# RWKV-7 recurrence and a low-rank mixer on one core: the recurrence's inverse, products and order written anew

## The chip, the core and the metric

The kernel runs on one core of one Trainium2 chip. TensorE (PE) multiplies, VectorE (DVE), ScalarE (ACT) and GpSimd (POOL) do the elementwise work, and SyncE (SP) issues the DMAs. The metric is the device time of one execution in microseconds (us), smaller is better. Everything is computed in float32.

## The reference

```python
# r, k, v, w, a, b: (4 batches, 8 heads, 768 steps, 40)
for t in range(S):
    y[t]  = r[t] @ state                      # state: (B, H, 40, 40)
    Sa    = state @ a[t]
    state = state * w[t] - outer(Sa, b[t]) + outer(v[t], k[t])
x = y as (B, 768, 320)                        # heads side by side
u = x + (x.T @ U @ V).T                       # U: (768, 32), V: (32, 768)
out = u + relu(u @ w_ch1) @ w_ch2             # (320, 1280), (1280, 320)
```

The weights of the mixer come as 64-bit floats and are turned into float32 on the core, from their halves, in pieces of 320 columns.

## The kernel before

**Units.** The steps are cut into 12 chunks of L = 64, the batches into two pairs. A *unit* is one chunk of one pair, with its 8 heads; there are N = 24 units, 0 to 11 for the first pair. Within a chunk the recurrence is written with the running product P of the decays: keys and b are divided by P, a and r multiplied by it, and the steps inside the chunk become products of 64x64 matrices per head and batch: a strictly triangular matrix is masked, the inverse T of identity minus a triangle is needed, and only the 40x40 state passes from unit to unit.

**Stages of a unit.** `prep_f` (L273) clips w, turns it (`up`, four transposes with the identity, L253), makes P by one scan of 512 columns (L289), turns P back twice (pp, pq, L258), takes 1/P with RECIPROCAL (L296), makes bt on POOL (L312), turns it and multiplies it with `fa` (`scores`, L264): `fn`, the negative triangle, which goes to DRAM (`fd`) and comes back as `ln`, with each 16x16 diagonal block on one partition, 64 lanes a unit. `substitute` inverts these blocks on POOL for two units at once: 14 steps of two operations (L348, L350). The result goes over DRAM (`TD`) and back (`fetch`) into `tc`. `prep_s` widens the inverse from 16 to 32 (pg, px, L398 and L420, 32x32 products) and from 32 to 64 (pg2, px2, L436 and L446), turns v, r and kt, and makes the masked scores `e` and `cm`. `carry` uses the state: ph (L463, L468), pX (L477), py (L485, L490), pg, pd (L509), the output py with ng (L528), which L530 multiplies by `qt` into XTM. The new state is decayed on DVE (L520), doubled on POOL into ST (L523) and turned by eight transposes into pS (L537).

**Quarters.** A product of 64 rows and 64 columns fills one quarter of the array. `scores` walks the quarters (0,0), (1,1), (0,1), (1,0); the loops over `hs` use row half x with output half x, so only two of the four.

**Order.** A generator yields between the steps, and `merged` weaves carry of unit n, prep_s of n+1, prep_f of n+5 and substitute by fixed shares; the queues of all engines follow that text:

```python
            merged(*gens)
            next(wload, None)
            if n >= 0:
                next(wload, None)
```

SP's queue in particular takes loads, fd, ln, TD and tc in this order. PSUM has four one-bank tiles and two two-bank tiles.

**Between the halves.** The squares of all inputs and outputs (L247) are counted against limits; `flag` is read by every engine (L603), and only if a limit is passed is the recurrence run again step by step (L604). It isn't in these runs. Then the mixer: `mix` (U, V, turns), `up_proj` (L729, L732) and `down_proj` (L744, L748), six groups of four units, 512 columns at a time.

Of the kernel before, what the change touches and what calls it, by code (L numbers as in the profile page):

```python
# [15 lines left out]
W_LO, W_HI = 0.6, 1.6  # L32
X_HI = 1e5
Y_HI = 1e18
# [3 lines left out]
def kernel(  # L38
# [22 lines left out]
    DP = 64  # L61
    LB = 16
    N = NB // 2 * NCH
    NCHK = 7
    NJ = DFF // 128
    WP = 320

    def half(x):
        return slice(64 * x, 64 * (x + 1))


    gl = ctx.enter_context(tc.tile_pool(name="gl", bufs=1))
    ones = gl.tile([128, 128], F32, name="ones")
    nc.vector.memset(ones[:], 1.0)
    ID = gl.tile([128, 128], F32, name="ID")
    nc.gpsimd.affine_select(out=ID[:], in_=ones[:], pattern=[[1, 128]], compare_op=ALU.is_equal,
                            fill=0.0, base=0, channel_multiplier=-1)

    MU = gl.tile([128, L], F32, name="MU")
    MF = gl.tile([128, L], F32, name="MF")  # L80
    IB = gl.tile([128, 32], F32, name="IB")
    up_ = gl.tile([128, 1], F32, name="up_")
    with tc.tile_pool(name="build", bufs=1) as bp:
        m = bp.tile([128, 128], F32, name="m")
        nc.gpsimd.affine_select(out=m[:], in_=ones[:], pattern=[[1, 128]], compare_op=ALU.is_gt,
                                fill=0.0, base=0, channel_multiplier=-1)
        f = bp.tile([128, 128], F32, name="f")
        nc.gpsimd.affine_select(out=f[:], in_=ones[:], pattern=[[LB, 128 // LB], [0, LB]],
                                compare_op=ALU.is_gt, fill=0.0, base=0, channel_multiplier=-1)
        for x in range(2):  # L90
            nc.vector.tensor_copy(MU[half(x), :], m[half(x), half(x)])
            nc.vector.tensor_copy(MF[half(x), :], f[half(x), half(x)])
    for q in range(4):
        s = slice(32 * q, 32 * q + 32)
        nc.vector.tensor_copy(IB[s, :], ID[s, s])
        nc.vector.memset(up_[s, :], 1.0 - q % 2)


    XTM = gl.tile([128, N, DM], F32, name="XTM")
    flag = gl.tile([1, 1], I32, name="flag")  # L100
    U_, V_ = gl.tile([128, NCH, RANK], F32, name="U_"), gl.tile([RANK, T], F32, name="V_")

    W1 = [gl.tile([128, DFF], F32, name=f"W1_{i}") for i in range(3)]
    W2 = gl.tile([128, NJ, DM], F32, name="W2")

    def weights(pool):

        u = moe_U.rearrange("(c p) k -> p c k", p=L)
        for c in range(0, NCH, 6):
            x = slice(c, c + 6)  # L110
            yield from piece(pool, U_[:, x, :], [(half(h), u[:, x, :]) for h in range(2)])
        for t in range(0, T, WP):
            x = slice(t, min(t + WP, T))
            yield from piece(pool, V_[:, x], [(slice(0, RANK), moe_V[:, x])])
        for f in range(0, DFF, WP):
            x = slice(f, f + WP)
            for i in range(2):
                yield from piece(pool, W1[i][:, x], [(slice(0, 128), moe_w_ch1[128 * i:128 * i + 128, x])])
            yield from piece(pool, W1[2][:, x], [(half(h), moe_w_ch1[256:320, x]) for h in range(2)])
        w2 = moe_w_ch2.rearrange("(j p) e -> p j e", p=128)  # L120
        for j in range(NJ):
            yield from piece(pool, W2[:, j, :], [(slice(0, 128), w2[:, j, :])])

    def piece(pool, dst, srcs):

        p = dst.shape[0]
        n = dst.size() // p
        if srcs[0][1].dtype == F32:  # L130
            for s, x in srcs:
                nc.sync.dma_start(out=dst[s], in_=x)
            yield
            return
        raw = pool.tile([128, WP, 2], I32, name="raw", bufs=2)
        x = raw[:, 0:n, :].rearrange("p n h -> p (n h)")
        if len(dst.shape) == 3:
            x = x.rearrange("p (j e) -> p j e", j=dst.shape[1])
            dst = dst.rearrange("p j e -> p (j e)")
        for s, y in srcs:  # L140
            nc.sync.dma_start(out=x[s], in_=y.bitcast(I32))
        yield
        raw = raw[0:p, 0:n, :]
        lo, hi = raw[:, :, 0], raw[:, :, 1]
        t = pool.tile([128, WP], I32, name="bits")[0:p, 0:n]
        e = pool.tile([128, WP], I32, name="unit")[0:p, 0:n]
        s = pool.tile([128, WP], I32, name="size")[0:p, 0:n]
        g = pool.tile([128, WP], F32, name="low")[0:p, 0:n]
        nc.scalar.activation(out=g, in_=lo.bitcast(U32), func=ACTF.Copy, scale=2.0 ** -52)  # L149
        nc.vector.tensor_scalar(out=t, in0=hi, scalar1=3, scalar2=0x3FFFFFF8,  # L150
                                op0=ALU.logical_shift_left, op1=ALU.bitwise_and)
# [6 lines left out]
                                op0=ALU.is_ge)  # L158
        nc.gpsimd.tensor_tensor(out=g, in0=t.bitcast(F32), in1=g, op=ALU.add)
        nc.gpsimd.tensor_tensor(out=dst, in0=g, in1=e.bitcast(F32), op=ALU.mult)  # L160
        yield

    with ExitStack() as p1:
# [172 lines left out]
        def substitute(u):  # L339
# [4 lines left out]
            for j in range(1, LB - 1):  # L344
# [6 lines left out]
                if j % 2:  # L351
                    yield
# [438 lines left out]
```

## Time and profile before

| | |
|---|---|
| Time, median of 3 runs | 1075.54 us (1068.68 to 1079.84) |
| Profiled execution, first to last instruction | 1071.0 us |
| PE busy | 903.6 us, 84% |
| DVE, ACT, POOL busy | 330.3, 251.7, 300.4 us |
| Mean granted PE clock | 0.835 of full |
| First and last XTM output (L530) | 95.5 and 705.2 us |
| Largest groups | L744 135.8 us, L729 111.0 us (PE) |
| DMA | 51.19 MB, 26.4% of the 16 engines |

The profile is of one execution and gives its span, not its time as the runs are timed; the runs lie around the span by what happens before the first and after the last instruction. A group of instructions is given as line, engine, output<-input, partitions x elements, count, busy time and mean. A float32 product appears as two records, a transpose as one. PE's busy time is not its speed: the granted clock beside it, in tenths of full, says how fast it ran.

### The profile page before, as it was taken

How to read it: one execution, taken by the hardware profiler on the slowest of the kernel's cores; microseconds unless marked ns; L12 is line 12 of the kernel's file. 1: busy time of each engine (PE TensorE's matmuls, PEld its weight loads, DVE VectorE, ACT ScalarE, POOL GpSimd, SP SyncE). 2: the span in 40 equal slices, each digit the busy share in tenths (PEclk: the TensorE clock that was granted, in tenths of full speed). 3: DMA queues.
4: the chain of work that ended last, by engine and by line, in shares of the span. 5: the costliest groups of instructions: out<-in, count | busy, mean ns of one | idle time of the engine just before them, and what ended most of it. 6: DMA issues, size and time to landing. Idle time of an engine off the chain costs nothing. (4 is left out here: it accounts for less than half of the span.)

```text
span 1071.0 us, 33742 instructions
## 1 busy us (share of the span) xinstructions
PE 903.6 (84%) x15146; PEld 675.0 (63%) x15146; DVE 330.3 (31%) x668; ACT 251.7 (23%) x630; POOL 300.4 (28%) x616
## 2 busy tenths in 40 slices
PE   2558789888788888888997868978989999999988
PEld 2447688777677787776886857853636455454635
DVE  5534334354434445443434214111111110101010
ACT  1223333333433343333333323200000000000010
POOL 5434524453625353525244446000000000000000
PEclk9656777787868787867779668669999999999999
DMA  4464342535252525443525221000000001010001
GB/s 97 70 96 80 50 85 42 95 48 99 45 99 45 96 48 99 70 73 51 94 42 91 51 61 27 3 3 0 13 13 13 12 1 25 1 24 1 22 3 25
DMA packets 262500, 51.19 MB, mean 48 GB/s; under 512 B 256112, under 2 KB 259216, under 8 KB 262352
## 3 DMA queue, kind: packets, MB, share of 16 engines
q1 hardware_dynamic: 262352, 49.01, 26.4%
q8 instruction: 119, 1.95, 0.7%
q14 instruction: 29, 0.24, 0.1%
HBM read 36.11 MB, written 12.86 MB: 46 GB/s over the span
## 5 line engine op out<-in xcount | busy, mean ns | idle before, releaser
L744 PE MATMUL p<-W,hid 128*128 128x320 f32 x480 | 135.8, 438 | 0.0
L729 PE MATMUL p<-uf,W 128*128 128x512 f32 x240 | 111.0, 605 | 16.6 <-ACT hid L734 16.6
L744 PEld LDWEIGHTS p<-W,hid 128*128 128x128 f32 x480 | 89.2, 190 | 45.3 <-issue 11.3
L729 PEld LDWEIGHTS p<-uf,W 128*128 128x128 f32 x240 | 43.1, 189 | 82.3 <-issue 45.8
L734 ACT ACTIVATE hid<-p 128x512 f32<-128x512 f32 x30 | 17.9, 597 | 324.1 <-PE p L732 324.1
L537 PE MATMUL pS<-ID,ST 128*128 128x128 f32 x176 | 43.9, 419 | 35.0 <-POOL ST L523 35.0
L296 DVE RECIPROCAL ip<-pp 128x320 f32<-128x320 f32 x24 | 51.8, 2158 | 46.1 <-PE pp L258 46.0
L735 DVE TENSOR_SCALAR hid<-p 128x512 f32<-128x512 f32 x30 | 20.8, 692 | 139.4 <-PE p L732 139.4
L537 PEld LDWEIGHTS pS<-ID,ST 128*128 128x128 f32 x176 | 35.2, 221 | 37.1 <-POOL ST L523 36.8
L436 PE MATMUL pg<-tt,fm 32*64 32x32 f32 x768 | 43.1, 277 | 13.1 <-DVE tt L428 11.6
L751 DVE TENSOR_TENSOR o<-p,XTM 128x320 f32<-128x320 f32 x24 | 11.8, 492 | 136.8 <-PE p L748 136.8
L436 PEld LDWEIGHTS pg<-tt,fm 32*64 32x64 f32 x768 | 40.0, 203 | 17.5 <-PE px L420 8.1
L156 POOL TENSOR_TENSOR low<-low,unit 128x320 f32<-128x320 f32 (+3 forms) x27 | 22.4, 829 | 100.9 <-ACT low L149 75.9
L350 POOL TENSOR_TENSOR ln<-ln,tmp 128x14 f32<-128x14 f32 (+6 forms) x168 | 45.4, 271 | 11.9
L348 POOL TENSOR_TENSOR tmp<-ln 128x14 f32<-128x14 f32 (+6 forms) x168 | 44.7, 266 | 12.7
L150 DVE TENSOR_SCALAR bits<-raw 128x320 int32<-128x320 int32 (+3 forms) x27 | 17.1, 634 | 96.4 <-DMA raw<-in_moe_w_ch_dram 75.2
L287 DVE COPY seg<-pw 128x8 f32<-128x8 f32 x24 | 4.1, 171 | 132.5 <-PE pw L253 132.5
L523 POOL TENSOR_TENSOR ST<-sc,slot 128x640 f32<-128x640 f32 x22 | 27.6, 1255 | 57.8 <-DVE sc L520 57.8
L446 PEld LDWEIGHTS px<-t,GX 32*64 32x64 f32 x768 | 39.3, 194 | 7.0 <-issue 4.8
L446 PE MATMUL px<-t,GX 32*64 32x32 f32 x768 | 43.7, 271 | 0.0
L312 POOL TENSOR_TENSOR nBT<-nB,ip 128x320 f32<-128x320 f32 x24 | 20.7, 863 | 77.3 <-DVE ip L296 72.4
L463 PE MATMUL ph<-nV,e 64*64 64x40 f32 x768 | 41.1, 282 | 0.0
(155 smaller groups left out, 1660.6 us busy)
## 6 DMA issues: line engine op xcount, KB each, us to landing
fd<-fn SPq DMA_DIRECT2D x48, 128.0 KB, 2.6
raw<-in_moe_w_ch_dram SPq DMA_DIRECT2D x18, 320.0 KB, 4.0
nW<-in_w_dram SPq DMA_DIRECT2D x48, 80.0 KB, 3.1
nA<-in_a_dram SPq DMA_DIRECT2D x48, 80.0 KB, 3.0
nB<-in_b_dram SPq DMA_DIRECT2D x48, 80.0 KB, 2.9
nR<-in_r_dram SPq DMA_DIRECT2D x48, 80.0 KB, 2.8
nK<-in_k_dram SPq DMA_DIRECT2D x48, 80.0 KB, 3.2
nV<-in_v_dram SPq DMA_DIRECT2D x48, 80.0 KB, 3.2
```

Of the source, the lines that this page charges most:

```text
L156: nc.gpsimd.tensor_tensor(out=g, in0=g, in1=e.bitcast(F32), op=ALU.mult)
L296: nc.vector.reciprocal(out=u.ip[:], in_=heads(p[:])[:, :, 0:D])
L348: nc.gpsimd.tensor_tensor(out=x, in0=ln[:, 0:j, j:j + 1].to_broadcast([128, j, n]), in1=ln[:, j:j + 1, j + 1:].to_broadcast([128, j, n]), ...
L350: nc.gpsimd.tensor_tensor(out=ln[:, 0:j, j + 1:], in0=ln[:, 0:j, j + 1:], in1=x, op=ALU.add)
L436: nc.tensor.matmul(out=pg[half(x), 32 * h:32 * h + 32], lhsT=fm[s, h, :], rhs=tt[s, h, :], start=True, stop=True)
L446: nc.tensor.matmul(out=px[half(x), 32 * h:32 * h + 32], lhsT=GX[s, h, :], rhs=t2[s, h, :], start=True, stop=True)
L463: nc.tensor.matmul(out=ph[half(x), s, i], lhsT=u.e[half(x), s, i, :], rhs=vt[half(x), 2 * i + s, 0:D], start=i + s == 0, stop=first, skip_ ...
L523: nc.gpsimd.tensor_tensor(out=ST[:, :, :, 0:D], in0=sc[:].rearrange("p i x e -> p (i x) e").unsqueeze(2).to_broadcast([128, NH, 2, D]), in ...
L537: nc.tensor.transpose(out=p[:, h // 4, 128 * (h % 4):128 * (h % 4 + 1)], in_=ST[:, h].rearrange("p s e -> p (s e)"), identity=ID[:])
L729: nc.tensor.matmul(out=ps_[x][:], lhsT=W1[i][:, (j + x) * 128:(j + x + 1) * 128], rhs=uf[i][:], start=(i == 0), stop=False)
L735: nc.vector.tensor_scalar_max(hid[:, j + 1, :], ps_[1][:], 0.0)
L744: nc.tensor.matmul(out=p[:, 0:DM], lhsT=hid[:, f, 2 * j * L:2 * (j + 1) * L], rhs=W2[:, f, :], start=(f == 0), stop=False, skip_group_chec ...
```

## The change

The recurrence, its order and the mixer are written anew; the fallback behind the flag stays.

- **Order.** Nothing is issued where it is written: each step is added to a list (`Plan.add`) with engine, planned duration, priority and buffers, and `Plan.order` runs one list schedule over all engines, PSUM places included; the queues follow it. PSUM is four pairs of banks, given out by the plan.
- **P and 1/P.** w is taken in packed rows of 320 columns; its check is one ACT pass. A backward scan gives the products of the later decays, their total is inverted (five columns), and a forward scan gives P. RECIPROCAL over 320 columns, the clip and the squares go.
- **Inverse.** 32x32 diagonal blocks lie on lanes, 32 lanes a unit, in groups of up to four units: 30 steps of two operations, on DVE for unit 0 alone, on POOL for the other seven groups. tLN and tLT have one buffer. T1 and T2 widen 32 to 64.
- **Products** of 64x64 walk all four quarters (QUADS). The state is one tile, decayed on DVE, turned by 16 products (SP).
- **Slots.** Eight sets of prepared operands, four of them in the room of W2 and of the mixer's tile MX; units 20 to 23 use the four others, so W2 is loaded after unit 15 through a single conversion buffer.
- **Mixer.** Groups of three units, 384 columns. x plus the low-rank part is written to XTM first. The half for the first pair has priority 1000, and may use up to four banks while units remain; the second half has 2000. The flag is read at the very end.

```diff
+LAT = {"PE": 160.0, "DVE": 110.0, "ACT": 130.0, "POOL": 120.0, "SP": 2500.0}
...
+                while free[e] <= t and ready[e]:
+                    pick = None
+                    for pri, n in sorted(ready[e]):
+                        o = self.ops[n]
...
+                    if e == "PE":
+                        if o.mode != mode:
+                            d += 95
+                        mode = o.mode
+                    o.start, o.end = t, t + d
+                    free[e] = o.end
...
+    pairs = [ps.tile([128, 2, 512], F32, name=f"pb{i}") for i in range(4)]
...
+    tLN, tLT = ring("tLN", 1, 1024), ring("tLT", 1, 1024)
...
+    CV = ring("CV", 1, 2 * WP, I32)
...
+    PARTS = (("aT", 512), ("NN", 512), ("KQ", 512), ("BQ", 512), ("Pn", TP))
+    SLOT = sum(c for _, c in PARTS)
+    NPERM, NSL = 4, 8
...
+    room = [[W2F, 0, NJ * DM], [MX, 0, MXC]]
...
+        return slots[n % NSL if n < 20 else n - 20]
...
+    QUADS = ((0, 0), (1, 1), (0, 1), (1, 0))
...
+    GROUPS = [[0], [1, 2, 3]] + [list(range(n, n + 4)) for n in range(4, 20, 4)] + [[20, 21], [22, 23]]
...
+        PL.add("PE", 400, f, r=[W], w=[pw], pri=pri, mode=1, name=f"wT{n}")
+        PL.add("ACT", 650, lambda: act(JK[:], W.ap[:], func=ACTF.Relu, scale=-1.0, bias=WLO[:],
+                                       accum_out=SQ[:, n:n + 1]), r=[W], w=[whole(JK), PL.buf(SQ, n, n + 1)],
...
+        PL.add("DVE", 180, lambda: nc.vector.memset(pw.ap[:, 0:NS + 1:L], 0.0), r=[pw], w=[pw], pri=pri, name=f"z{n}")
+        PL.add("DVE", 800, lambda: nc.vector.tensor_tensor_scan(
+            out=RB.ap[:, ::-1], data0=pw.ap[:, 1:NS + 1][:, ::-1], data1=C1[:, ::-1], initial=0.0,
+            op0=ALU.mult, op1=ALU.add), r=[pw], w=[RB], pri=pri, name=f"bs{n}")
+        w0 = whole(tW0)
+        PL.add("DVE", 180, lambda: nc.vector.tensor_tensor(out=tW0[:], in0=RB.ap[:, 0:NS:L], in1=WF.ap[:, 1:NS:L], op=ALU.mult),
+               r=[RB, WF], w=[w0], pri=pri, name=f"pl{n}")
+        PL.add("DVE", 180, lambda: nc.vector.reciprocal(out=D1.ap[:, 0:NS:L], in_=tW0[:]),
+               r=[w0], w=[D1], pri=pri, name=f"rc{n}")
+        PL.add("DVE", 800, lambda: nc.vector.tensor_tensor_scan(
+            out=FW.ap, data0=WF.ap, data1=D1.ap, initial=0.0,
+            op0=ALU.mult, op1=ALU.add), r=[WF, D1], w=[FW], pri=pri, name=f"fs{n}")
...
+            for y in range(2):
+                for x in range(2):
+                    mm(pp.ap[half(x), y, 0:128], FW.ap[:, 128 * x + 64 * y:128 * x + 64 * y + 64], ID[:])
+            for y in range(2):
+                for x in range(2):
+                    mm(pp.ap[half(x), y, 128:160], FW.ap[half(y), 256:320], ID[half(y), 64 * y + 32 * x:64 * y + 32 * x + 32])
+        PL.add("PE", 560, f, r=[FW], w=[pp], pri=pri, mode=1, name=f"Pn{n}")
...
+                        mm(pl.ap[half(h2), 4 * y + 2 * l:4 * y + 2 * l + 2], S["Pn"].ap[:, c0:c0 + 64], E0[:])
+        PL.add("PE", 300, f, r=[S["Pn"]], w=[pl], pri=pri + 2, mode=2, name=f"PL{n}")
...
+        turned(S["aT"], AH, pri, f"aT{n}")
+        turned(BT, S["BQ"], pri, f"BT{n}")
+        pf = P2()
+        scores_a(pf, BT, S["aT"], pri, f"F{n}")
+        masked(S["NN"], pf, MN, pri, f"NN{n}")
...
+    HEADS = [(x, y, l, h2) for x in range(2) for l in range(2) for y, h2 in QUADS]
+    HEADC = [(x, y, l, h2) for x in range(2) for h2 in range(2) for y, l in QUADS]
+
+    def scores_a(p, bt, at, pri, name):
+        def f():
+            for x, y, l, h2 in HEADS:
+                c0 = 128 * (2 * x + l)
+                mm(p.ap[half(y), h2, c0 // 2:c0 // 2 + 64], bt.ap[half(h2), 256 * l + 128 * x + 64 * y:256 * l + 128 * x + 64 * y + 64],
+                   at.ap[half(h2), 256 * y + 128 * l + 64 * x:256 * y + 128 * l + 64 * x + 64])
+        PL.add("PE", 500, f, r=[bt, at], w=[p], pri=pri, mode=3, name=name)
...
+        eng, e = (nc.vector, "DVE") if g == 0 else (nc.gpsimd, "POOL")
+        tm = whole(tTM[0])
+        for j in range(1, 31):
+            m = 31 - j
+
+            def f(j=j, m=m):
+                y = tTM[0][0:nl, 0:j * m].rearrange("p (a b) -> p a b", b=m)
+                eng.tensor_tensor(out=y, in0=x3[0:nl, 0:j, j:j + 1].to_broadcast([nl, j, m]),
+                                  in1=x3[0:nl, j:j + 1, j + 1:].to_broadcast([nl, j, m]), op=ALU.mult)
+                eng.tensor_tensor(out=x3[0:nl, 0:j, j + 1:], in0=x3[0:nl, 0:j, j + 1:], in1=y, op=ALU.add)
+            c = 400 + 3.5 * j * m if e == "POOL" else 350 + 2.0 * j * m
+            PL.add(e, c, f, r=[ln], w=[ln, tm], pri=pri - 4, name=f"lan{g}.{j}")
...
+        PL.add("POOL", 220, lambda: nc.gpsimd.memset(ln.ap[0:nl, 0:1024:33], 1.0), r=[ln], w=[ln], pri=pri - 4, name=f"dg{g}")
+        PL.add("ACT", 1150, lambda: act(lt.ap[0:nl].rearrange("l (t j) -> l t j", j=32),
+                                        x3[0:nl].rearrange("l j t -> l t j")), r=[ln], w=[lt], pri=pri - 4, name=f"LT{g}")
+        gd = gdram[g % 2]
+        gdb = gd_buf[g % 2]
+        for blk, s in ((1, ln), (0, lt)):
+            PL.add("SP", 430, lambda blk=blk, s=s: dma(
+                gd[0:nl // 2, blk].rearrange("l j t -> l (j t)"), s.ap[blk:nl:2]),
+                r=[s], w=[gdb], pri=pri - 4, grp=("gd", g), name=f"gd{g}")
...
+            for h in range(NH):
+                for x in range(2):
+                    s = slice(64 * x, 64 * x + 32)
+                    mm(p.ap[half(x), 32 * h:32 * h + 32], S["NN"].ap[s, 64 * h:64 * h + 64], AB.ap[s, 32 * h:32 * h + 32])
+        PL.add("PE", 500, f, r=[S["NN"], AB], w=[p], pri=pri, mode=4, name=f"T1.{n}")
...
+        for h2 in range(2):
+            p = P2()
+
+            def f(h2=h2, p=p):
+                for i in range(4):
+                    h = 4 * h2 + i
+                    for y in range(2):
+                        for blk in range(2):
+                            rows = slice(64 * y + 32 * blk, 64 * y + 32 * blk + 32)
+                            mm(p.ap[half(h2 ^ y), blk, 32 * i:32 * i + 32], LT2.ap[rows, 64 * h:64 * h + 64],
+                               ID[rows, rows] if blk == 0 else AB.ap[rows, 32 * h:32 * h + 32])
+            PL.add("PE", 330, f, r=[LT2, AB], w=[p], pri=pri, mode=4, name=f"T2.{n}.{h2}")
...
+        turned(KT, S["KQ"], pri, f"KT{n}")
+        pe, pc = P2(), P2()
+        scores_a(pe, KT, S["aT"], pri, f"E{n}")
+        masked(E, pe, MU, pri, f"mE{n}")
+        turned(VT, V, pri, f"VT{n}")
+        turned(RT, R, pri, f"RT{n}")
+        scores_r(pc, lambda x, y, l, h2: 128 * (2 * x + h2) + 64 * y, VT, RT, pri, f"C{n}")
+        masked(C, pc, MU, pri, f"mC{n}")
+
...
+                        mm(ph.ap[half(q), y, D * i:D * i + D], S["aT"].ap[half(h2), a0:a0 + 64],
+                           ST.ap[half(h2), 160 * y + D * i:160 * y + D * i + D])
+            PL.add("PE", 400, f, r=[S["aT"], ST], w=[ph], pri=pri, mode=3, name=f"H{n}")
+            PL.add("DVE", 520, lambda: nc.vector.scalar_tensor_tensor(
+                out=nh, in0=ph.ap[:, :, 0:160], scalar=-1.0, in1=ne, op0=ALU.mult, op1=ALU.add),
+                r=[ph, NE], w=[NHh], pri=pri, name=f"eH{n}")
...
+            for t, z in ((C, S["KQ"]), (G, S["BQ"])):
+                for l in range(2):
+                    for h2 in range(2):
+                        for x, y in QUADS:
+                            c0, k0 = 256 * l + 64 * (2 * x + h2), 256 * l + 128 * x + 64 * h2
+                            mm(py.ap[half(x), y, 80 * l + D * h2:80 * l + D * h2 + D], t.ap[half(y), c0:c0 + 64],
...
+            PL.add("DVE", 500, lambda: decay(st4, pd.ap[:, :, 0:160].rearrange("p s (i d) -> p s i d", d=D)),
+                   r=[pd, pls], w=[ST], pri=pri, name=f"S0.{n}")
+        else:
+            PL.add("DVE", 420, lambda: decay(st4, SN.ap.rearrange("p (s i d) -> p s i d", s=2, d=D)),
...
+                    mm(p.ap[32 * gq:32 * gq + 32, x, 0:DM], U_[half(x), c, :], XTM[half(x), pr * NCH + c, :],
+                       start=c < 4, stop=c >= 8)
+        PL.add("PE", 2000, f, r=bU + [xtm[n] for n in units], w=[p], pri=pri, mode=5, name=f"ph{pr}")
...
+                        mm(p.ap[half(x), y, 0:DM], V_[s, (c + y) * L:(c + y + 1) * L], hut.ap[s, DM * x:DM * x + DM])
+            n0 = pr * NCH + c
+            PL.add("PE", 700, f, r=bV + [hut], w=[p], pri=pri + 0.01 * c, mode=6, name=f"V{pr}.{c}")
...
+                            mm(p.ap[:, y, 0:GN], W1[i][:, (j + y) * 128:(j + y + 1) * 128], ufs[i].ap, start=i == 0, stop=False)
+                        prev = (PL.add("PE", 650, f, r=[ufs[i]] + [bW1[x, i] for x in fs], w=[p], pri=q + 0.02, mode=0,
+                                       grp=("up", pr, g, j), name=f"up{pr}.{g}.{j}", after=prev),)
+
+                def f(j=j, p=p):
+                    for y in range(2):
+                        mm(p.ap[:, y, 0:GN], W1[2][half(y), (j + y) * 128:(j + y + 1) * 128], ufs[2].ap[half(y)], start=False)
+                PL.add("PE", 700, f, r=[ufs[2]] + [bW1[x, 2] for x in fs], w=[p], pri=q + 0.02, mode=7, grp=("up", pr, g, j),
+                       name=f"up{pr}.{g}.{j}", after=prev)
...
+                        mm(p.ap[:, 0:DM], hid.ap[:, f_ * GN + 128 * jj:f_ * GN + 128 * jj + 128], W2[:, f_, :],
+                           start=f_ == 0, stop=f_ == NJ - 1)
+                    prev = (PL.add("PE", 545, f, r=[hidj[f_ // 2], bW2[f_]], w=[p], pri=q + 0.04, mode=0, grp=("dn", n),
+                                   name=f"dn{n}", after=prev),)
...
+    for g, us in enumerate(GROUPS):
+        for u, n in enumerate(us):
+            q = us[0] - 4.6 + 0.35 * u
+            load(n, "WABK", q - 1)
+            prep_f(n, q, lane[n])
+        lanes(g, us[0] - 4.6)
+        if g == 0:
+            weights1(1.0, 0.8)
+        if us[0] == 16:
+            weights2(16.0, 0.5)
+        for n in us:
+            load(n, "VR", n - 2.5)
+            prep_t(n, lane[n], n - 1.5)
+            prep_s(n, n - 1.2)
+            carry(n, n)
+        if us[-1] == 19:
+            mixer(0, 1000.0, True)
+    mixer(1, 2000.0, True)
+
...
+    steps, span = PL.order(4, 4)
+    global PLAN
+    PLAN = PL, steps, span
+    with tc.manual_schedule():
+        for o in steps:
+            o.fn()
+    main.close()
...
-            for i, s, x in hs:
-                nc.tensor.matmul(out=ph[half(x), s, i], lhsT=u.e[half(x), s, i, :], rhs=vt[half(x), 2 * i + s, 0:D],
-                                 start=i + s == 0, stop=first, skip_group_check=True)
...
-        for n in range(-AH, N):
...
-            merged(*gens)
...
-    uf = mix(0)
-    for g in range(NG):
-        hid = up_proj(uf)
-        if g + 1 < NG:
-            uf = mix(g + 1)
-        down_proj(g, hid)
```

## The prediction

> **What bounds the kernel now.** I read the forty slices first, then cut the span where the work changes, then looked at single blocks of TensorE.
>
> ```profile
> PE   2558789888788888888997868978989999999988
> PEclk9656777787868787867779668669999999999999
> ```
>
> PE is busy nearly everywhere, but its clock has two regimes: 0.6 to 0.8 up to slice 26, 0.9 and more after it. The cuts of the second view are the first output of a unit (95.5 us), the last one (705.2), and the first matmul of the mixer (711.2):
>
> ```profile
> core 0: us, PE busy (x) PEld busy (x) DVE busy (x) ACT busy (x) POOL busy (x), PEclk, DMA share, GB/s
> 95.50:705.20 609.70, 515.88 (x13084) 459.26 (x13084) 237.01 (x483) 206.77 (x530) 257.85 (x498) 0.76 0.37 63
> 0.00:95.50 95.50, 48.58 (x812) 41.53 (x812) 44.75 (x102) 26.99 (x70) 42.58 (x118) 0.75 0.51 87
> 705.20:711.20 6.00, 0.19 (x2) 0.09 (x2) 1.51 (x8) 0.00 (x0) 0.00 (x0) 0.50 0.02 5
> 711.20:1071.00 359.80, 338.95 (x1248) 174.14 (x1248) 47.03 (x76) 17.92 (x30) 0.00 (x0) 0.99 0.05 11
> ```
>
> So 1071.0 = 95.5 lead + 609.7 for 23 further units (26.5 each) + 6.0 for flag and branch + 359.8 mixer. No other engine is over 43% in the second row, and the mixer is TensorE at full clock. The waits of PE between 100 and 700 us are small but for one:
>
> ```profile
> PE pS L537 <- POOL ST L523: 35.0, 11, 9.1
> PE pd L509 <- DVE ng L269: 12.2, 16, 0.8
> PE px L420 <- issue: 11.6, 9, 2.1
> PE pg L436 <- DVE tt L428: 10.6, 10, 1.2
> ```
>
> The price of a block is its start to the next start, at the full clock and at the half clock (columns: start, length, then the group):
>
> ```profile
> 230.75 0.66 PE L258 MATMUL pp<-ID,PF 128*128 128x128 f32 x4
> 231.24 0.60 PE L258 MATMUL pq<-ID,PF 128*128 128x128 f32 x4
> 231.77 0.69 PE L264 MATMUL pg<-fr,xf 64*64 64x64 f32 x32
> 232.28 0.65 PE L264 MATMUL pe<-fa,fk 64*64 64x64 f32 x32
> 232.75 0.65 PE L264 MATMUL pe<-fr,fv 64*64 64x64 f32 x32
> ...
> 694.11 1.93 PE L463 MATMUL ph<-nV,e 64*64 64x40 f32 x32
> 695.97 1.33 PE L468 MATMUL ph<-ST,fa 128*64 128x80 f32 x16
> ```
>
> A product is two records. At the full clock four transposes take 0.49, and 16 products on all four quarters 0.47. The same 16 in `hs` order, which meets only the two diagonal quarters, took 1.06 (py at 228.98 to 230.04) and at the half clock 1.86 (the ph row). The other full-clock starts: pd 0.49 per 16 products, ph and py with 80 columns 0.6 to 0.7, pg and px of 32x32 blocks 0.8, pg2 and px2 on two row groups 1.05.
>
> **TensorE work of a unit, at the full clock.** Before: 44 transposes 11 x 0.49 = 5.4; five score blocks and pX 2.35; pd 1.0; ph, py, py again 3.2; the 80-column products 1.3; pg, px 1.6; pg2, px2 2.1: 16.9 us. The chip spent 515.9/23 = 22.4 busy us on it, a factor 1.33 (clock 0.76), and 26.5 of span, another 1.18 of waits.
>
> After: prep_f: aT, BT 1.0; wT, Pn, Q, each two transposes or four half-width products and four small ones, 0.45 to 0.5; the PL pairs 0.5 (below); F 0.47: 3.4. prep_t: T1 has L446's two row groups and half its products (16 for two blocks of 8): by that row 1.05, T2 two four-quarter blocks 0.95: 2.0. prep_s: three turns, E, C: 2.4. carry: He, H, X, XT, G, Yr, SP seven at 0.47, Y and S two each: 5.2. Sum 13.0, with first and last chunks shorter 12.8. So 24 units cost 307 us at the full clock instead of 406: 99 less, or 132 at this stage's clock. The doubtful items: PL (16 records with two columns) lies between 0.2 (records at the 14.5 ns spacing of L264) and 0.7 (the 80-column row), I take 0.5; T1 between 0.47 and 1.9 (L436 at the half clock), I take 1.05; reversed operands in the scan: none in the trace, between nothing and a second 1.22 us of DVE, which is hidden.
>
> **The clock: rule against row.** The Trainium skill, "TensorE: Matmul & The Clock Gate", Part 1, says that the array reaches full rate after about one busy window of 3.4 us; a denser stage would then pay no 1.33. The trace disagrees for these small products:
>
> ```profile
> 456.00:466.00 10.00, 10.00 (x164) 9.10 (x165) 2.98 (x8) 4.54 (x11) 3.07 (x5) 0.72 0.55 85
> 483.00:503.00 20.00, 18.55 (x480) 16.64 (x472) 7.80 (x14) 6.55 (x17) 10.33 (x28) 0.77 0.37 58
> ```
>
> PE is 100% and 93% busy there, at 0.72 and 0.77. By the rule units cost 12.8 x 1.09 = 14.0, by the row 12.8 x 1.33 x 1.09 = 18.6. I take the row. The 1.09 for waits is my choice, half of the 1.18: the ST wait (35 of about 90 us) goes, since the state is made on DVE and needs no doubled ST and no pS; the other hops stay.
>
> **What is hidden.** POOL:
>
> ```profile
> L350 POOL TENSOR_TENSOR ln<-ln,tmp 128x56 f32<-128x56 f32 x24 | 7.4, 308 | 1.9
> L350 POOL TENSOR_TENSOR ln<-ln,tmp 128x14 f32<-128x14 f32 x24 | 5.2, 218 | 1.1
> L348 POOL TENSOR_TENSOR tmp<-ln 128x56 f32<-128x56 f32 x24 | 7.0, 291 | 1.8
> L348 POOL TENSOR_TENSOR tmp<-ln 128x14 f32<-128x14 f32 x24 | 5.1, 213 | 1.8
> ```
>
> Some 188 ns and 1.86 or 2.14 ns an element. The 30 steps have 4960 elements in each of two operations: 60 x 188 + 4960 x 4.0 = 31 us a group. Seven groups 217, AH and eY 94 operations of 160 elements (0.53 each) 50, conversion 27 x 1.75 = 47: with memsets 325 us, against PE's 460 over that time. The skill's "GPSIMD Engine Reference", section 4.1, says elementwise work belongs on VectorE, being about twice as fast: this speaks against 217 us of it here. On DVE it would be an estimated 108 by that factor; by the rows POOL has the room, so the sum of the kernel is the same either way while POOL is off the path. If the cover goes, the price is rival 3. DVE loses the 2.16 us reciprocal, clip and check, 3.3 us a unit, ACT five squares and their readouts, also 3.3, all beside PE: nothing. SP issues 12 loads, 2 nd, ln, 2 AB, 2 out a unit, 0.4 to 0.65 us each: 12 us, under 18.6, and nd waits for NN with loads queued behind it, as fd did for fn (66 us of SP waiting).
>
> **The lead.** Unit 0 after 9 us of preamble and load: scans, P, AH, turns, F and mask with hops 12; nd and ln to and from DRAM 7.5 (landings of 2.6 and 2.7); its 30 steps on DVE 20 (no row; by the POOL rows at half price, bounds 16 and 31); LT, gd, AB 9; T1, T2: 63 us to its first X. tLN and tLT are single buffers, so group 1 loads its lanes only after group 0's gd (54), computes 31 on POOL and has T at **104**. By then PE has done some 40 us (full-clock) of prep_f for eight units and unit 0. The next groups need 31 + 12 other POOL work + 7 for the round trip = 50 us per four units, below PE's 74.
>
> **The sum.** Units 0 to 15: 104 + (16 x 12.8 - 40) x 1.45 = 343. From there W2's room is free, its ten pieces go through the single CV, some 8 us each, so half of the mixer can use the gaps only partly for 80 us: I add 10. Mixer in full: up 8 x 5 x (4 x 0.68 + 1.3) = 161 (0.925 and 1.74 measured at 512 columns, here 384), down 240 x 0.558 = 134, turns 10, ph, RS, V in quarters 15 instead of 15 + 38: 320, 160 a half, against 360. Units 16 to 23: 102 x 1.2 (half of the clock loss, since the dense matmuls lie between them) = 123. So 343 + 123 + 160 + 10 = 636; the second half needs unit 23's output: 8 for ph, copies and RS in series, 160, then 4 for output, flag and branch, now at the very end: **808**. The median of the runs lies 4.5 above the profiled span: **812**. The gap of 6.0 before the mixer goes; the flag is computed under it.
>
> **Rivals.** (1) *The clock follows density*, as the rule has it: 104 + 165 x 1.09 = 284, then 102 + 160 + 10, then 172: 728, 732 timed. For: slices at 0.9 in the mixer; against: the two rows above. Mixed cases lie at 740 to 770. (2) *The half of the mixer does not get in early*: 104 + 267 x 1.45 = 491, + 6 + 320 + 12 = 829, 834 timed. It is only 22 more, since PE does the same work: the fill saves waits and clock, not products. (3) *POOL is the bound*: were the wide lane steps twice the rows (82 us a group), unit 15 would end near 430 and all near 900; only from about 74 us a group does it decide. (4) *Slower*: **the one list order stalls TensorE**. Every engine runs its queue in the order of a plan with fixed durations (0.40 to 0.50 a block, full clock); where the chip differs, PE stands at the head of its queue for a block while others are ready. A unit has some 31 PE blocks. Slower than before begins where each waits 0.55 us (17 us a unit: 104 + 22.5 x 35.6 = 905, mixer half inside, + 172); with the 0.65 that lies under one ng hop (0.8 in the waits), 20 a unit: 977 + 172 = 1150. For: ng and tt hops of 0.8 to 1.2 exist now; against: eight slots of prepared units give the list other work, and real PE is slower than planned, so others come early.
>
> **Numbers.** Forecast, 770 to 860 with rival 2 inside: 0.57. Rival 1 and its mixtures, under 770: 0.22. Rival 3 and lesser stalls, 860 to 1060: 0.10. Rival 4: 0.09, no change 0.02. Range 728 to 900, from rival 1 to rival 3. A measurement of this kernel tells about 1% from no change.
>
> **Right or wrong by:** first XTM output near 65 to 75, unit 1 near 110; 18 to 19 us a unit until 343; clock 0.75 to 0.8 there, 0.9 later; `dn` of the first half before unit 23's Y; the last 160 us a dense mixer; lane steps near 0.22 to 0.7 us; no PE wait above 35 us in total. Wrong if PE is under 80% busy between 110 and 640, or the clock there is over 0.9.

## The result, and the profile after

The changed kernel takes 962.6 us (median of four runs, 956.9 to 969.2), the kernel before in the same comparison 1072.4 (1068.7 to 1079.8). The ratio is 0.897, interval 0.891 to 0.902: 110 us faster, where 263 were forecast. 962.6 lies above the range of 728 to 900.

The forty slices of the changed kernel (columns: 24.0 us each, tenths):

```profile
PE   3749728979889897885989277965999999999996
...
POOL 4002757544561664464216867132000000000000
PEclk9755957876896988887699768996899999999999
```

Counted from 0, PE has holes in slice 5 (120 to 144 us, the lead), 18, 22 (528 to 552, two tenths), 26 and 27 (624 to 672). Past the lead, the kernel before had none under six tenths. POOL is at 6 to 8 tenths in slices 21 to 24. The same stages cut out (the stretches are the lead, units of steady pace, a stretch with late units, and the last 360 us in three parts):

```profile
core 0: us, PE busy (x) PEld busy (x) DVE busy (x) ACT busy (x) POOL busy (x), PEclk, DMA share, GB/s
0.00:150.00 150.00, 91.32 (x1708) 71.50 (x1708) 81.08 (x202) 43.70 (x91) 57.12 (x124) 0.69 0.55 95
150.00:430.00 280.00, 238.32 (x8111) 206.51 (x8109) 115.76 (x246) 100.94 (x212) 148.65 (x280) 0.82 0.45 82
500.00:550.00 50.00, 31.27 (x1132) 26.27 (x1129) 15.82 (x34) 14.19 (x29) 36.05 (x72) 0.86 0.20 38
600.00:640.00 40.00, 36.60 (x762) 23.67 (x761) 14.58 (x33) 10.49 (x19) 9.68 (x14) 1.00 0.19 48
640.00:680.00 40.00, 22.18 (x42) 11.78 (x43) 11.26 (x29) 2.47 (x5) 9.50 (x11) 0.66 0.15 46
680.00:960.00 280.00, 260.31 (x1046) 149.40 (x1044) 33.84 (x57) 23.63 (x34) 0.00 (x0) 0.99 0.06 14
```

Between 500 and 550 PE is busy 63% and POOL 72%: the units do not run at PE's pace there. Between 640 and 680 PE is busy 55%, and no unit is left. The chain that ended last says what it stood for (start, length, what ran):

```profile
638.99 0.89 POOL CG L871
639.95 0.87 POOL CG L873
641.36 2.85 DMA CV<-in_moe_w_ch_dram
644.60 0.50 DVE W L864
645.60 0.89 POOL CG L871
646.56 0.87 POOL CG L873
647.45 0.50 DVE W L875
647.97 2.95 DMA CV<-in_moe_w_ch_dram
...
674.36 28.23 PE pb L438 x88
```

Along this chain one piece of the second weight matrix is a load into `CV`, steps of DVE, two steps of POOL and a last one of DVE, and the next load waits for that last one: 6.6 us a piece (641.36 to 647.97), in series, until 674. The mixer's `dn` needs all ten. The waits, kernel-wide, show the same chain from its other end (us in total, times, longest):

```profile
POOL CG L871 <- DVE CV L867: 106.7, 17, 11.4
POOL XTM L778 <- DVE tYS L774: 75.6, 21, 7.4
...
POOL tAH L517 <- ACT slot L431: 41.3, 13, 9.9
PE pb L438 <- issue: 35.2, 37, 2.1
...
PE pb L438 <- DMA tAB<-gd: 28.6, 5, 13.8
```

POOL stands 107 us at a conversion step at the head of its queue, until a load and DVE's steps are done. The lanes lose little by it: in five of the seven groups on POOL the first step starts within 0.2 us of the landing of its operand `ln` (222.3 after 222.1, for instance). The cost lies in the other direction. A lane group runs 41 to 59 us on POOL, and a conversion step that stands behind it waits for all of it. The 27 pieces of the weights are done 6 to 16 us apart, but for six intervals of 42 to 74 us (146 to 203, 214 to 288, 315 to 372, 381 to 447, 510 to 552 and 558 to 605), and a lane group runs in each of these.

PE's longest single wait in the kernel is the hole of slice 22. The view of waits puts it down to L945, the addition after the mixer's first products with `V`. But what stands at the head of PE's queue is the work of a unit: T1 of unit 20 (`tAB,slot`), with the next products with `V` behind it.

```profile
534.67 0.77 PE L438 MATMUL pb<-MX,V__63 32*64 32x320 f32 x8 [0.79 <-ACT MX L431]
558.71 1.80 PE L438 MATMUL pb<-tAB,slot 32*64 32x32 f32 x27 [23.28 <-DVE XTM L945]
```

The chain in that window shows what was late:

```profile
528.32 0.56 POOL tTM L607
528.95 0.64 POOL tLN L609
...
548.74 0.31 POOL tLN L609
549.81 1.97 ACT tLT L431
...
556.62 0.47 POOL CG L871
557.16 0.46 POOL CG L873
557.64 0.29 DVE V__63 L875
557.94 0.75 DVE XTM L945
558.71 1.37 PE pb L438 x19
```

T1 needs `tAB`, the inverse of unit 20 from the lane group that runs on POOL until 549. Its two halves landed from DRAM at 558.6 and 558.9, and L945 ended at 558.7 between them: the wait is put down to L945 by a tenth of a microsecond. The same lane group holds up the conversion of the last pieces of `V`, which were done at 552 and 558. So units 20 and 21 leave a gap, and the mixer, whose work was to fill it, has no inputs yet. The run without the fill, below, has the same gap.

**Where the forecast's 152 us went** (808 of span against 960.4, by marks read off the trace: the first X of unit 1, the last Y of unit 15, the first product with `U` of the second half of the mixer):

| stretch | forecast | measured | error |
|---|---|---|---|
| to the first X of unit 1 (forecast: its T) | 104 | 149 | +45 |
| on to unit 15 | 239 | 289 | +50 |
| on to the second half of the mixer | 293 | 353 | +60 |
| to the end | 172 | 169 | -3 |

### The profile page after: what moved, and what is told of

The parts are those of the page before. It is cut to its first block, busy times and chain, and to the rows that moved or that the text cites. A ratio compares the mean times of both kernels' runs of the same rounds, so it can differ in the third digit from the quotient of the medians.

```text
span 960.4 us, 34791 instructions
## 1 busy us (share of the span) xinstructions
PE 772.0 (80%) x15706; PEld 565.7 (59%) x15706; DVE 318.1 (33%) x698; ACT 229.6 (24%) x456; POOL 316.3 (33%) x606
## 4 chain that ended last, share of the span: by engine, by line
PE 71%; DVE 9%; issue 6%; POOL 5%; DMA 4%; ACT 4%; SPq 0%; DVEq 0%; ACTq 0%; POOLq 0%
PE pb L438 62%; PE pb L435 9%; DMA CV<-in_moe_w_ch_dram 2%; POOL tLN L609 2%; POOL tTM L607 2%; DMA tAB<-gd 1%; DVE tTM L607 1%; DVE tLN L609 1%; DVE MX L1002 1%; ACT tLT L431 1%; DVE IC L314 1%; POOL CG L871 1%; POOL CG L873 1%; ACT tKT L431 1%; DVE slot L512 1%
## 5 line engine op out<-in xcount | busy, mean ns | idle before, releaser
L438 PE MATMUL pb<-W,MX 128*128 128x320 f32 x480 | 147.2, 460 | 28.7 <-DVE W L875 20.2
L438 PE MATMUL pb<-MX,W 128*128 128x384 f32 (+1 forms) x480 | 147.0, 514 | 0.0
L438 PEld LDWEIGHTS pb<-W,MX 128*128 128x128 f32 x480 | 92.1, 198 | 79.8 <-DVE W L875 25.1
L607 POOL TENSOR_TENSOR tTM<-tLN 128x84 f32<-128x84 f32 (+37 forms) x210 | 103.9, 495 | 37.9 <-DMA tLN<-nd 23.3
L609 POOL TENSOR_TENSOR tLN<-tLN,tTM 128x84 f32<-128x84 f32 (+37 forms) x210 | 109.5, 522 | 16.5
L438 PEld LDWEIGHTS pb<-MX,W 128*128 128x128 f32 (+1 forms) x480 | 70.6, 190 | 73.1 <-issue 41.7
L431 ACT ACTIVATE MX<-pb 128x768 f32<-128x768 f32 (+4 forms) x52 | 33.7, 649 | 274.3 <-PE pb L438 170.5
L438 PE MATMUL pb<-tAB,slot 32*64 32x32 f32 x512 | 23.2, 241 | 47.1 <-DVE XTM L945 23.3
L438 PE MATMUL pb<-ID,tLT 32*64 32x32 f32 x768 | 33.4, 257 | 5.8 <-issue 2.9
L438 PEld LDWEIGHTS pb<-ID,tLT 32*64 32x64 f32 x768 | 29.7, 174 | 12.8 <-issue 5.9
L438 PE MATMUL pb<-tAB,tLT 32*64 32x32 f32 x768 | 33.6, 257 | 1.5 <-issue 1.5
L438 PEld LDWEIGHTS pb<-ID,tFW 128*64 128x64 f32 (+1 forms) x384 | 19.4, 167 | 21.4 <-issue 18.6
L438 PEld LDWEIGHTS pb<-tAB,tLT 32*64 32x64 f32 x768 | 29.9, 173 | 0.1
```

What stands on the lines that cost most here:

```text
L431: nc.scalar.activation(out=o, in_=i, func=kw.pop("func", ACTF.Copy), **kw)
L438: nc.tensor.matmul(out=o, lhsT=l, rhs=x, start=start, stop=stop, skip_group_check=True)
L607: eng.tensor_tensor(out=y, in0=x3[0:nl, 0:j, j:j + 1].to_broadcast([nl, j, m]), in1=x3[0:nl, j:j + 1, j + 1:].to_broadcast([nl, j, m]), op ...
L609: eng.tensor_tensor(out=x3[0:nl, 0:j, j + 1:], in0=x3[0:nl, 0:j, j + 1:], in1=y, op=ALU.add)
```

## The experiments

My theory on seeing this: **(A)** the plan's fixed durations for TensorE are too short (its own list holds 589 us of TensorE work, the trace 772), so the list places the weights' steps too late and queues them behind others. The rival: **(B)** POOL is the bound, its conversion and lane steps delay each other, and the plan is innocent. Further: **(C)** the lead's DRAM round trips; **(D)** TensorE's own pace in the units. Times are medians of several runs, ratios are against the kernel before on the same chip. The runs were on different chips, so a difference of two medians is good to some 10 us: where the text has 45, 70, 48, 28 and 15 us, the ratios (0.897 for the changed kernel) give 40, 63, 46, 19 and 19. "Up0" is the start of the mixer's first `up`, "W2" the end of the second weights' last piece; the changed kernel has 595 and 674.

**Honest durations for TensorE in the plan.** Only the order of instructions changes, none is added or taken.

```diff
                     if e == "PE":
+                        if o.pri < 999:
+                            d *= 1.35
...
```

> Only the planned durations change: every TensorE step of the units is planned 1.35 times as long, as the profile after shows them; the same operations in another list order. Theory A (the list order was made for a faster TensorE, so that queues stand at heads that come late): 860 to 910 us. Rival B (lane steps held up on POOL by other POOL work, whatever the durations): within 1% of 962. Rival C (TensorE itself is the bound of the units): within 1% of 962.

917.2 us, ratio 0.860 (0.854 to 0.865): 45 less. Unit 15 ends at 436 as against 438, so the units are not better ordered. What comes earlier are the weights: W2 at 632, up0 at 541. Order alone is worth 45 us, and by these marks through the weights.

**POOL for the lanes only.** `AH`, `eY` and the two conversion steps go to DVE.

```diff
-            PL.add("POOL", 480, lambda y=y: nc.gpsimd.tensor_tensor(
+            PL.add("DVE", 330, lambda y=y: nc.vector.tensor_tensor(
...
-        PL.add("POOL", 150 + 710 * ks, lambda: nc.gpsimd.tensor_tensor(out=gg, in0=gg, in1=lo.bitcast(F32), op=ALU.mult),
+        PL.add("DVE", 150 + 420 * ks, lambda: nc.vector.tensor_tensor(out=gg, in0=gg, in1=lo.bitcast(F32), op=ALU.mult),
...
```

> The products with P (AH, eY) and the two POOL steps of the weight conversion go to VectorE, so POOL has only the lane steps. Planned durations of TensorE as in the changed kernel. Rival B: the lane groups fall from 41 to 59 us to about 32 and the loop over the eight slots from 83 to about 65 us per four units: 860 to 900 us. Theory A alone: 930 to 960. Rival C: within 1% of 962.

892.1 us, ratio 0.838 (0.833 to 0.844): 70 less, the fastest of the kernels that compute everything. Its windows for the two stretches that were holes, and for the units:

```profile
150.00:430.00 280.00, 235.60 (x8343) 203.31 (x8331) 163.08 (x364) 106.99 (x226) 118.45 (x224) 0.88 0.48 90
500.00:550.00 50.00, 45.42 (x837) 29.27 (x835) 31.68 (x57) 14.33 (x25) 36.37 (x70) 0.93 0.27 59
...
640.00:680.00 40.00, 37.99 (x153) 22.28 (x153) 4.64 (x8) 4.38 (x7) 0.00 (x0) 1.00 0.07 16
```

PE is busy 91% and 95% where it was 63% and 55%; W2 is done at 544 and up0 starts at 492. Unit 15 ends at 419, 19 earlier. POOL, now with nothing but lanes, needs 36 us a group; in the changed kernel a group took 41 to 59. Neither A nor B is decided by these two: both act on the weights.

**Only the conversion off POOL**, so that B falls apart in its halves.

```diff
...
-        PL.add("POOL", 150 + 710 * ks, lambda: nc.gpsimd.tensor_tensor(out=gg, in0=d, in1=gg, op=ALU.add),
+        PL.add("DVE", 150 + 420 * ks, lambda: nc.vector.tensor_tensor(out=gg, in0=d, in1=gg, op=ALU.add),
```

> Only the two POOL steps of the weight conversion (CG at L871 and L873) go to VectorE; the products with P stay on POOL. If the 70 us of the run with lane steps alone came from the weights, which then were ready at 544 us and let the first mixer half into the units: 885 to 910 us, W2 done by 560. If they came from AH and eY leaving the lane steps' queue: 940 to 960 us.

914.5 us, ratio 0.854 (0.846 to 0.861): 48 of the 70. Up0 at 467, W2 at 555; unit 15 at 436, all but unchanged. So some two thirds of what POOL cost was the weights' conversion behind lane steps, and not the lanes' supply to the units. The hole of slice 22 is gone with it, though the lane group of units 20 and 21 takes as long as before (46 us, 520 to 566): the mixer's products lie there now, and PE is 93% busy from 520 to 566.

**No fill at all**: both halves of the mixer after the last unit.

```diff
...
         if us[-1] == 19:
-            mixer(0, 1000.0, True)
+    mixer(0, 1000.0, True)
```

> The first half of the mixer starts only after the last unit. If the fill is empty in the changed kernel because W2 is converted late (674 us, 40 us after the last unit), this costs nothing: 955 to 975 us. If the fill was worth what the forecast gave it (about 22 us): 980 to 1000 us.

977.7 us, ratio 0.914 (0.906 to 0.922): the fill as placed is worth 15 us. Rival 2 put the whole fill at 22. The edit also answers whose the hole of slice 22 is. No product with `V` is in PE's queue before the last unit now, and T1 of unit 20 still comes after 25.4 us of idle PE, put down to `tAB<-gd`. The groups of T1 on the two pages, the changed kernel's first (the last figures are all of PE's idle time before T1 and the largest part of it):

```profile
L438 PE MATMUL pb<-tAB,slot 32*64 32x32 f32 x512 | 23.2, 241 | 47.1 <-DVE XTM L945 23.3
```

```profile
L438 PE MATMUL pb<-tAB,slot 32*64 32x32 f32 x512 | 24.9, 251 | 68.7 <-DMA tAB<-gd 66.8
```

**No loading of W2**: each piece is a memset (loading and conversion of the second weights are left out).

```diff
-            piece(W2[:, j, :], bW2[j], [(slice(0, 128), w2[:, j, :])], pri)
+            PL.add("DVE", 400, lambda j=j: nc.vector.memset(W2[:, j, :], 0.0), w=[bW2[j]], pri=pri, name="w2z")
```

> Leaves out loading and converting W2: it is set to zero as soon as its room is free. If the late W2 is what keeps the first mixer half out of the units: 860 to 900 us, with the first down projections near 520 us and the units' pace as before. If TensorE has no room between the units' work anyway: 920 to 940 us, the 40 us of waiting alone.

934.5 us, ratio 0.879 (0.871 to 0.887): 28 less, and up0 still at 596. Before it come the products with `V`, which need the last of the first weights, and these go through the same buffer (done at 559 here, 558 in the changed kernel). W2 alone is 28; the whole of the late weights is more.

**The lead.** Units 0 to 3 become one group, whose lanes run on DVE, so that unit 1 does not wait for a second trip through DRAM.

```diff
-    GROUPS = [[0], [1, 2, 3]] + [list(range(n, n + 4)) for n in range(4, 20, 4)] + [[20, 21], [22, 23]]
+    GROUPS = [list(range(n, n + 4)) for n in range(0, 20, 4)] + [[20, 21], [22, 23]]
```

> Only the lane groups change: units 0 to 3 in one group on VectorE. The changed kernel has unit 0 at 88 us and then waits for unit 1 until 149. With one group the four should start near 125 and follow each other: if the lead's 40 us of the forecast's miss lie in that second group, 935 to 950 us; if the later loop absorbs it, within 1% of 962.

960.9 us, ratio 0.896 (0.889 to 0.904): no change. Unit 1's X comes at 127 instead of 149, unit 7 ends at 273 as against 277. The 22 us are given back within six units: the next lane group, that of units 4 to 7, ends at 197 as against 199, and PE stands 12.8 us for it. The lead was mis-sized by 45, but the time behind it is not lost in full. This group of four took 22.4 us on DVE; on POOL with nothing but lanes it takes 36, 1.6 times as long. All lane steps on DVE is an obvious version that was not run.

**More TensorE work in the units**: the four score blocks (E, F, C and G) are computed twice, each into the same place.

```diff
-            for x, y, l, h2 in HEADS:
+            for x, y, l, h2 in HEADS + HEADS:
...
-            for x, y, l, h2 in HEADC:
+            for x, y, l, h2 in HEADC + HEADC:
```

> The changed kernel with the four score blocks of a unit (F, E, C, G) run twice into the same place: 64 more products a unit, 2.2 us at the full clock, 53 us over 24 units; same list order. If TensorE's work bounds the units: 1010 to 1030 us, and the last unit near 690. If the units wait elsewhere and the clock only sags in the pauses: 965 to 980 us, with the granted clock of the units up from 0.82 to 0.88 or more, as in the run with two quarters.

1032.7 us, ratio 0.963 (0.953 to 0.972): 70 more. The four doubled blocks measure 1.09 to 1.16 at the full clock, about 0.55 more each, 2.2 a unit, 53 in all. The pace between units 3 and 15 goes from 20.8 to 24.3 us. 53 us at the full clock are 63 at the 0.84 granted, and 70 were paid: nothing hides TensorE's work, (D) holds.

**Fewer lane steps**: 2 of 30 (28 are left out).

```diff
-        for j in range(1, 31):
+        for j in range(1, 3):
```

> Leaves out 28 of the 30 steps of the inverse on the lanes, so a lane group takes 2 us instead of 41 to 59. If the lanes and their loop set the pace: unit 15 ends near 340 and the kernel takes 800 to 840 us. If TensorE's queue does: unit 15 ends above 400, and the kernel takes 870 to 900 (the weights, free of the lane steps, come early as in the run with POOL's lane steps alone).

879.7 us, ratio 0.818 (0.811 to 0.825). The windows of this kernel, of the one with doubled scores, and of the changed one (above) in the same stretch:

```profile
150.00:430.00 280.00, 245.69 (x7858) 211.72 (x7850) 132.12 (x305) 104.28 (x228) 58.16 (x97) 0.80 0.53 97
```

```profile
150.00:430.00 280.00, 232.88 (x8277) 203.64 (x8277) 105.71 (x227) 87.26 (x182) 125.58 (x240) 0.84 0.44 79
```

POOL's load falls from 149 us to 58 and the units do not come faster: 21.8 us each from unit 3 to 15 (20.8 before the edit). What it gains lies at both ends: unit 1's X at 116, and unit 23's last Y at 576 instead of 635. The profiled execution took 895.7 us, 2% over the median, so its pace is an upper reading. Between units 3 and 15 the lanes do not set the pace, and rival 3 is wrong; late in the loop they do leave gaps, as before unit 20.

**Seven slots** of prepared units instead of eight. (Later units' operands are overwritten in this version, so it is read to unit 15 only.)

```diff
-    NPERM, NSL = 4, 8
+    NPERM, NSL = 4, 7
```

> Seven sets of prepared operands instead of eight; W2's room then is free only after unit 18, so the total says little and the pace up to unit 15 is read. If the loop over the slots (unit done, prep_f of the unit eight later, DRAM, lanes, DRAM, carry) sets the pace: unit 15 ends near 490 instead of 438. If TensorE's queue sets it: 438 to 450.

Unit 15 ends at 482 instead of 438. PE does less in the same stretch:

```profile
150.00:430.00 280.00, 209.81 (x6820) 182.16 (x6818) 109.59 (x242) 89.94 (x189) 132.19 (x239) 0.77 0.45 81
```

238 busy us become 210: one slot less starves TensorE. The total, 1048.1 from two runs (ratio 0.975, 0.962 to 0.987), is told for completeness. The prepared units do the work that the prediction gave them against rival 4.

**Two quarters at a time**: the eight product steps of `carry` (ten blocks of 16 products) run over one pair of quarters and then over the other.

```diff
-            for i in range(4):
-                for y, h2 in QUADS:
...
+            for i, y, h2 in two(4):
...
```

> The changed kernel with the eight product blocks of carry in the order of the kernel before: first all products of the two diagonal quarters, then all of the two others; same products, same list order. By the rows of before a block of 16 takes 1.06 instead of 0.47 us at the full clock, 10 blocks a unit, 5 to 6 us a unit. If TensorE's work bounds the units: 1040 to 1110 us, with 25 us a unit. If the loop over eight slots (lane steps, trips to DRAM) bounds them: 975 to 1000 us.

968.7 us, ratio 0.906 (0.900 to 0.913): unchanged within the intervals. A block takes 0.53 to 0.86 at the full clock, start to next start, instead of 0.47 to 0.60; that is less than the 1.06 of the kernel before, whose order leaves all 16 products on two quarters where this one leaves eight. So this is no full undo of that part. Still the blocks cost more, and none of it appears in the pace (186 to 437 us, 20.9). The window shows where it went:

```profile
150.00:430.00 280.00, 245.89 (x8094) 217.72 (x8092) 115.03 (x244) 101.11 (x212) 147.90 (x277) 0.88 0.45 82
```

As many instructions, 7.6 us more busy time, and a granted clock of 0.88 instead of 0.82. The product of both is 195 us at the full clock before and 216 now: 21 more, or 1.6 for each of the 13 units. Slower blocks came with a faster clock. What four quarters are worth in time is thereby not shown; the order of the kernel before was not tried.

**All together**: measured TensorE durations by block in the plan, conversion off POOL, the first group of four.

```diff
+PE_NS = {'wT': 690, 'Pn': 990, 'Q': 740, 'PL': 590, 'BT': 640, 'aT': 620, ...
...
```

> A version from the first four runs: TensorE planned with the measured duration of each step, the conversion's POOL steps on VectorE, and units 0 to 3 as one lane group on VectorE in place of 0 alone and 1 to 3 on POOL. Theory A and the weights add up: 840 to 870 us. If they are one and the same loss: 885 to 900 us.

896.4 us, ratio 0.837 (0.831 to 0.843). And **measured durations with POOL for the lanes only** (the edit of the second experiment, and this one):

```diff
+                        d = PE_NS.get(o.name.split(".")[0] if o.name[:2] in ("T1", "T2") else o.name.rstrip("0123456789."), d)
...
```

> POOL with the lane steps alone, as in the run that gave 892, and the list planned with the measured TensorE durations. If the order is still a loss there: 865 to 880 us. If it was the weights and POOL alone: 885 to 900.

907.1 us, ratio 0.844 (0.836 to 0.851). Neither beats POOL for the lanes only (0.838). The gains of 45 and 70 do not add: both undo the same loss. A and B are two ways to the same late weights, and each alone takes most of it away; which of the two is "the" cause has no answer here.

## Why the prediction was wrong, step by step

In short, two terms of the sum failed: the room that POOL was said to have, so that the weights came late (45 to 70 us by the runs that mend it), and the factor of 1.09 for waits (28 us by the rows). The lead was too short as well, by 45 us, but 22 us of it, taken away in a run, bought nothing.

**What bounds: right for the steady units, not for the whole.** From 150 to 430 PE works at its own pace, and in the mixer it is dense. Doubled scores cost more than their work; 28 of 30 lane steps do not change the pace. But over the stretch that the prediction named, PE is 78% busy, under the 80% that was to be its sign of being wrong:

```profile
110.00:640.00 530.00, 415.30 (x13229) 345.89 (x13220) 204.81 (x439) 170.61 (x350) 275.15 (x522) 0.81 0.38 72
```

The rest of the lead and the holes of slices 18 and 22 lie in it.

**The products: a term too small, 12.8 for 15.1 to 15.7.** By block, start to next start at the full clock: `wT` 0.61, `Pn` 0.84 and `Q` 0.66 (0.45 to 0.5 predicted each), turns 0.56 to 0.60 (0.49), E, F, C and G 0.52 to 0.64 and the products of `carry` 0.49 to 0.60 (0.47), `S` 0.95 and more (0.94), `Y` 0.96 and T1 1.05 (as taken), T2 0.55 a block (0.475). A part of the PE records of one unit (columns as in the prediction):

```profile
308.76 1.12 PE L438 MATMUL pb<-tAB,slot 32*64 32x32 f32 x32 [0.69 <-ACT tRT L431]
309.81 0.68 PE L438 MATMUL pb<-slot,tC 64*64 64x40 f32 x32
310.30 0.66 PE L438 MATMUL pb<-slot,tG 64*64 64x40 f32 x32
310.77 0.67 PE L438 MATMUL pb<-tRT,tVT 64*64 64x64 f32 x32
311.37 0.44 PE L435 MATMUL pb<-ID,tRB 128*128 128x128 f32 x2
```

The dense spacing of four-quarter blocks, 0.47 to 0.49 (309.81 to 310.30 to 310.77), was right. What I missed is the 0.1 that most other blocks cost over it, and the blocks of two shapes: `Pn` and `Q` alone are 0.5 over the sum. That it is the change of shape that costs is my reading; no run separates it.

**The clock: the right side, the factor too large.** 0.82 in the units, with PE busy 85% of 280 us. From 287 to 306.5 us PE is busy 93% and the granted clock is 0.50 all along. So the row decides: the rule that the prediction quotes, of full rate after a few busy microseconds, does not hold for these products, and rival 1 is wrong. But 17.7 busy us for 15.1 to 15.7 is a factor of some 1.15, where 1.33 was taken from a clock of 0.76. This miss and that of the products nearly cancel: 17.0 busy us a unit were forecast, 17.7 came.

**The 1.09 for waits: wrong.** A unit of 20.8 us (unit 3 to 15) holds 17.7 of busy PE: 1.175, where the row before had 1.18 and I chose half. The `ST` wait did go. What is left of PE's idle time from 150 to 430:

```profile
PE pb L438 <- issue: 23.0, 23, 2.1
PE pb L438 <- DMA tAB<-gd: 7.0, 2, 3.7
PE pb L438 <- ACT tBT L431: 1.5, 2, 1.0
```

More than half is "issue", mostly inside a block, and nothing that an earlier operand would mend. Stops fell from 4.1 us a unit to 3.1, in step with the work. 20.8 instead of 18.6 makes the forecast's 239 us 267, 28 of the 50 of the second row; the other 22 I cannot divide: the forecast charged that stretch with units 0 to 15 alone, while PE prepares later ones in it.

**The lead: 149 instead of 104.** For unit 0 it was 12 us from `NN` to its lanes (7.5 predicted) and 18 from lanes to T1 (9). The transfers are not all of it: `ln` landed 8 us after `NN` and the first step stood 3.6 more in DVE's queue; `AB` landed 12 us after the lanes and T1 stood 6 more in PE's. For the next group, unit 3's F came at 75, its `ln` at 85, and the first step at 92.7, behind an `AH` that waited at the head of POOL's queue. That group took 43 us (31 predicted); its steps alone are 31.0, as by the rows, and the rest is the time between steps and other work in the queue. And the lead matters less than I wrote: 22 us of it, taken away, bought nothing.

**The fill: the weights' way was not followed.** I gave W2 80 us from unit 15 on and added 10. The first weights were still on their way until 558, and W2 from 558 to 674. 6.6 us a piece is under the 8 I had; what made it late is that the pieces before 636 waited for lane steps and for the first weights. The room was not in the way: by the kernel's slots the part in W2 serves units 4, 5, 12 and 13, so it is free after unit 13 and not 15, and with the conversion off POOL the first piece of W2 is done at 430, before unit 15 ends. The step that failed is "by the rows POOL has the room": it has, as a sum (316 of 960 us), but not in the order of its queue. The runs that mend this one place, by order or by engine, gain 45, 48 and 70 us; of the 70, 51 come after unit 15, most of the +60 in the third row.

**Rival 4 named the mechanism, but for the wrong engine**: an engine stands at the head of its queue for a block while others are ready. It struck on POOL, where the conversion stood behind whole lane groups, instead of on TensorE for 0.55 a block; its price was a fifth of the one worked out (70 us, where rival 4 lay 338 over the forecast). TensorE's 23.3 us before unit 20 are not shown to be of this kind: the operand of the block at its head had just landed.

**The end: right.** From the second half on 169 us (172 predicted), a group of three units 38.2 (40 forecast, as 160 a half), the gap before the mixer gone.

**Rival 2 is what the mixer did**: its first half did not get in early. The 22 it gives the fill stands beside 15 measured without the fill; what it did not see is how much an early fill can take up: the gap before unit 20, and the 20 us that PE stood for W2 after unit 23.

## What to carry to other kernels

A written list of instructions is as good as the durations it was planned with: take them from a profile, at the clock that the chip grants, or the queue of one engine holds the work of another. Where work is to fill gaps, look for the chain that delivers its inputs (here weights, through one buffer and three engines) before counting the gaps. Where a profile names one releaser for a long wait, look when the instruction's other operands came, before blaming it. The factor for waits comes from the row, also where the largest wait in it goes away.

## What the runs showed that I had not expected

With slower blocks the granted clock in the same stretch was 0.88 instead of 0.82, and the time the same; one profiled execution of each shows it, and the kernel with POOL for the lanes only has 0.88 there too, with its blocks unchanged, so whether the one causes the other stays open. So does what PE's "issue" waits inside a block are. The best full version that was run, 892.1, is 70 us under the changed kernel and 80 over the forecast.
